# Turning gate columns and a product's operand by DRAM transfers and VectorE block transposes in an mLSTM and feed-forward kernel

## The chip, the core and the metric

The kernel runs on one core of a Trainium2 chip. A core has five engines that work side by side, each with its own queue of instructions in a fixed order: TensorE (PE; matrix products, with weight loads shown apart as PEld), VectorE (DVE), ScalarE (ACT), GpSimd (POOL) and SyncE (SP), which here only starts transfers. Transfers run on DMA engines. Operands lie in SBUF (128 partitions), products arrive in PSUM. The metric is the time of one execution on the device in microseconds.

## What is computed

Two blocks in a row, all in float32: an mLSTM cell with batch 4, 8 heads, 768 steps and head size 40, and a feed-forward block with 320 inputs, 2048 hidden units and 320 outputs on its 3072 rows.

```python
for t in range(S):
    m_new = np.maximum(f_gate[:, :, t] + m, i_gate[:, :, t])
    f_stab = np.exp(f_gate[:, :, t] + m - m_new)
    i_stab = np.exp(i_gate[:, :, t] - m_new)
    m = m_new
    C = f_stab[:, :, None, None] * C + i_stab[:, :, None, None] * np.einsum('bhd,bhe->bhde', vt, kt)
    n = f_stab[:, :, None] * n + i_stab[:, :, None] * kt
    h_tilde = np.einsum('bhde,bhe->bhd', C, qt)
    nq = np.einsum('bhd,bhd->bh', n, qt)[:, :, None]
    denom = np.maximum(np.abs(nq), 1.0)
    o = 1.0 / (1.0 + np.exp(-o_gate[:, :, t]))
    y[:, :, t] = o * h_tilde / denom
x = y.transpose(0, 2, 1, 3).reshape(B * S, H * D)
h = x @ w_in
g = h * (1.0 / (1.0 + np.exp(-1.702 * h)))
return g @ w_out
```

## The kernel before

The 768 steps are cut into six chunks of 128 (`w` = 0 to 5, called chunk 0 to 5 here). The sequential cell becomes, for each chunk, products of 128 by 128 or, from chunk 1 on, of two halves of 64 steps, with a carried state per head (`state`, and `state_mid` between the halves). All instructions are written in the order in which each engine runs them; there is no scheduler, and an engine waits at the head of its queue until its operands are there. All transfers are issued by SP, in program order, and completion counters are shared by every eighth transfer, so at most eight are under way.

The main loop runs over `w`. Each turn has an up stage (`up` for chunk 0, `up_fast` after it: `xT` times `w_in`, eight steps `j`, then GELU) and a down stage (`down`, 16 blocks, for chunk 0; `down_fast`, 14 blocks, after it: the hidden values times `w_out`). Between the blocks of the down stage of chunk `w` stands the attention of chunk `w + 1`, spread by the list `at` in `attention(w)`: a call at entry `i` comes after block `i`. So the attention of chunk 1 runs beside 16 blocks of chunk 0, and those of chunks 2 to 5 beside 14 blocks each. The last chunk has nothing beside its down stage.

The steps of an attention, in order:

- `gates(w)`, early in the up stage before: VectorE scans over the gates with heads on the partitions, stacked in `st` (96 rows: 32 heads by three quantities). From chunk 1 on the two halves of the steps are also copied the other way round into `swapped` (L290), and the decays between halves are spread by `dec` (L297). The running maximum goes to DRAM (`m_row`) and comes back spread over the partitions as `wt` (`spread`, eight transfers, L359).
- `columns(w)`: puts steps on the partitions. TensorE multiplies `st` by `keep` and `swapped` by `swap` (odd heads have their halves exchanged) and `dec` by `half`, into `p_cols` (L316, L317, L323). VectorE copies 32 columns (L326), ScalarE takes exponentials of the rest (L327, L329).
- `scale` (`vw`, L483) and `decay` (L476) on GpSimd; `weights` (32 exponentials on ScalarE, L377, and masks on GpSimd, L381); `carry` (TensorE `p_c` L493, then on VectorE L502, L476, L502 for each half of the heads); `scores` (TensorE `p_s` L401, VectorE L404); `values` (TensorE `p_o` L442 and `p_i` L450, then VectorE L456, L457 and `outputs`, which ends with `y`, L420, and a copy of 64 columns on GpSimd, L423).
- `seam`: TensorE transposes `y` in six pieces for each half of the batch into `p_x` (L466), ScalarE copies them to `xT` (L468).

`token_sums` (L555 to L560) forms sums of `xT` at the start of the next up stage, and `input_sums` (L544 to L547), in chunk 0's down stage only, sums of `w_in`: both are needed since `up_fast` and `down_fast` use seven products of halves where eight would be usual. `hidden_sums` (L663 to L666) and `last_sums` (L672) do the same for the down stage. Every block's result is added up by VectorE into `o_sb` (L690, L692; chunk 0: L640) and stored by SP (L696, L641).

PSUM is held by two pools. `ps_m` has four single banks for blocks and half of the up products. `ps_a` has two bank pairs (`banks(name)`), used in turn by p_cols, p_c, p_s, p_o, p_i, p_x and the rest of the up products; a user waits until the last reader of the pair two allocations before is done.

From chunk 2 on `k` and `q` are loaded as 32-row squares (`load_squares`, tiles `k_sq` and `q_sq`, issued after block 12) and turned by VectorE's block transposes of 32 by 32 (L349, in `block_transposes`). The calls that place all this in the main loop:

```python
at = (0, 1, 3, 4, 8, 9, 10, 11, 13) if w == 1 else (0, 1, 2, 4, 6, 7, 8, 9, 11)
calls = [[(columns, w), (decay, w, 0, 0), (decay, w, 1, 0), (scale, w, 0), (scale, w, 1)],
         [(weights, w, 0)], [(weights, w, 1), (open_gates, w)], [(carry, w, 0), (carry, w, 1)],
         [(scores, w, 0), (scores, w, 1)], [(values, w, 0)], [(values, w, 1)], [(seam, w, 0)], [(seam, w, 1)]]
```

Of the kernel before, what the change touches and what calls it, by code (L numbers as in the profile page):

```python
# [26 lines left out]
def kernel(  # L27
# [73 lines left out]
    def load_squares(w):  # L101
        for dst, src in ((k_sq, k), (q_sq, q)):
# [29 lines left out]
    def piece_in(c, n):  # L132
        return (w_in_sb[:, c, n * 512:(n + 1) * 512],
                [(slice(0, 128), slice(0, 512), w_in_bits[c * 128:(c + 1) * 128, n * 1024:(n + 1) * 1024])])
# [74 lines left out]
    keep, swap = (const.tile([3 * BH, 3 * BH], FP, name=n) for n in ("keep", "swap"))  # L209
    odd = const.tile([3 * BH, 1], FP, name="odd")  # L210
    full = ident[0:3 * BH, 0:3 * BH]

    half = const.tile([BH, 2, 64], FP, name="half")
    par = const.tile([BH, 2], FP, name="par")
    pair = const.tile([BH, BH // 2], FP, name="pair")
    V.tensor_reduce(out=par, in_=ident[0:BH, 0:BH].rearrange("p (j two) -> p two j", two=2), axis=AX.X, op=OP.add)
    V.tensor_reduce(out=pair, in_=ident[0:BH, 0:BH].rearrange("p (j two) -> p j two", two=2), axis=AX.X, op=OP.add)
    V.tensor_copy(out=half, in_=par.unsqueeze(2).to_broadcast([BH, 2, 64]))
# [7 lines left out]
    cols, stacked, m_row, dec = {}, {}, {}, {}  # L226
    kT, qT, ys, xT, gs, o_ps, sums, vw = {}, {}, {}, {}, {}, {}, {}, {}
# [16 lines left out]
    def gates(w):  # L244
# [42 lines left out]
        if w:  # L287
            stacked[w] = st, swapped
            for x in range(2):
                V.tensor_copy(out=swapped[:, x * HL:(x + 1) * HL], in_=st[:, (1 - x) * HL:(2 - x) * HL])  # L290
        if w:
            dec[w] = gate.tile([BH, 2, BH // 2], FP, name="dec")
# [3 lines left out]
            for x in range(2):  # L296
                V.tensor_scalar(out=dec[w][:, x, :], in0=pair, scalar1=both[:, x:x + 1], scalar2=None, op0=OP.mult)  # L297
# [8 lines left out]
    def masks():  # L306
        V.tensor_reduce(out=odd, in_=full.rearrange("p (j two) -> p two j", two=2)[:, 1], axis=AX.X, op=OP.add)
        V.tensor_scalar(out=swap, in0=full, scalar1=odd, scalar2=None, op0=OP.mult)
        V.memset(swap[BH:2 * BH, :], 0.0)
        V.tensor_tensor(out=keep, in0=full, in1=swap, op=OP.subtract)  # L310

    def columns(w):
        pt = banks("p_cols")[:, 0, :]
        st = stacked[w]
        if w:
            T.matmul(pt[:, 0:3 * BH], st[0], keep, start=True, stop=False)  # L316
            T.matmul(pt[:, 0:3 * BH], st[1], swap, start=False, stop=True)  # L317
        else:
            T.transpose(pt[:, 0:3 * BH], st, full)
        n = 3 * BH  # L320
        if w in dec:
            n += BH
            T.matmul(pt[:, 3 * BH:n], half.rearrange("p a b -> p (a b)"), dec[w].rearrange("p a b -> p (a b)"),  # L323
                     start=True, stop=True)
        c = cols[w] = gate.tile([L, 4 * BH], FP, name="cols")
        V.tensor_copy(out=c[:, 0:BH], in_=pt[:, 0:BH])  # L326
        A.activation(out=c[:, BH:3 * BH], in_=pt[:, BH:3 * BH], func=AF.Exp, scale=-1.0)  # L327
        if w in dec:
            A.activation(out=c[:, 3 * BH:n], in_=pt[:, 3 * BH:n], func=AF.Exp)  # L329
# [76 lines left out]
    def outputs(w, hs, u):  # L406
# [16 lines left out]
        G.tensor_copy(out=y[:, :, DM:DM + 64], in_=y[:, :, DM - 64:DM])  # L423
# [36 lines left out]
    def seam(w, c, bs=(0, 1)):  # L460
        if w not in xT:
            xT[w] = work.tile([128, 3, B, L], FP, tag="xT", bufs=1, name="xT")
        px = banks("p_x")[:, 0:len(bs), 0:3 * L]
# [386 lines left out]
```

## Time and profile before

| | value |
|---|---|
| median of three runs (lowest, highest) | 486.65 us (486.65, 486.92) |
| the profiled execution | 486.67 us |
| its span, first to last instruction | 485.0 us |
| granted TensorE clock | 1.00 |
| SP's hardware queue, share of 16 DMA engines | 50.3% |
| up stage of chunk 3, start to end | 270.5 to 303.1 us |
| down stage of chunk 3 | 303.1 to 344.6 us |
| DMA share in that up stage, in that down stage | 1.10, 0.05 |

A line of the profile's groups or timeline names the engine, the source line, what is written and read, shapes, and durations. "Idle before" is time in which the engine had nothing it could start, with the instruction that ended it. The chain of waits is the sequence of work that ended last, followed back from the end. Busy time of TensorE is modelled at the ends of pipelined products, so the chain's pieces are better for sums than the busy times.

### The profile page before, as it was taken

The page shows a single profiled execution, that of the slowest core. Times are in us where ns is not written, and L with a number is a line of the kernel's source. Part 1 is how long each engine was busy: PE and PEld are TensorE (multiplying, and loading weights), DVE is VectorE, ACT ScalarE, POOL GpSimd, SP SyncE. Part 2 cuts the span into 40 slices and gives each one's busy share as a digit, 9 for nine tenths or more (in the row PEclk, how much of TensorE's full clock was granted, in tenths as well). Part 3 has the DMA queues.
Part 4 walks back from the last instruction along what each step waited for, and adds up shares of the span by engine and source line. Part 5 has one row for each costly group of instructions (what it writes and reads, how often), then busy time and mean ns, then how long its engine had stood idle before and what let it go on. Part 6 is the DMA issues. An engine that isn't in the chain of part 4 may idle for free.

```text
span 485.0 us, 12103 instructions
## 1 busy us (share of the span) xinstructions
PE 479.3 (99%) x5016; PEld 388.0 (80%) x5016; DVE 344.0 (71%) x680; ACT 195.3 (40%) x434; POOL 149.7 (31%) x145
## 2 busy tenths in 40 slices
PE   8999999999999999999999999999999999999997
PEld 5774447777767999767999877999876999876997
DVE  6675976988778966768967668968677958343812
ACT  3746557801453901444811354720264630164200
POOL 6020003400398610127620136630035640035300
PEclk9999999999999999999999999999999999999999
DMA  8999995005992000999000899000799000000000
GB/s 176 182 285 146 254 206 153 2 18 103 208 157 45 3 30 3 174 185 139 1 31 3 153 189 158 1 31 3 127 195 165 10 30 3 29 0 1 0 28 27
DMA packets 130790, 44.31 MB, mean 91 GB/s; under 512 B 105616, under 2 KB 128176, under 8 KB 130736
## 3 DMA queue, kind: packets, MB, share of 16 engines
q1 hardware_dynamic: 130736, 43.55, 50.3%
q8 instruction: 39, 0.64, 0.6%
q14 instruction: 15, 0.12, 0.1%
HBM read 39.52 MB, written 4.01 MB: 90 GB/s over the span
## 4 chain that ended last, share of the span: by engine, by line
PE 95%; DVE 3%; POOL 1%; ACT 0%; issue 0%; POOLq 0%; DVEq 0%
PE p_out L687 32%; PE p_h L585 26%; PE p_h L590 8%; PE p_out L636 7%; PE p_h L515 6%; PE p_c L493 3%; PE p_o L442 2%; PE p_s L401 2%; PE p_i L450 2%; PE p_h L521 2%; PE p_x L466 1%; PE p_t L341 1%; PE p_o L432 1%; PE p_s L390 0%; DVE wt L392 0%
## 5 line engine op out<-in xcount | busy, mean ns | idle before, releaser
L627 POOL TENSOR_TENSOR g<-g,parts 128x512 f32<-128x512 f32 x30 | 38.3, 1276 | 124.4 <-DVE parts L619 113.3
L687 PE MATMUL p_out<-w_out_sb,g 128*128 128x160 f32 x480 | 71.0, 302 | 0.0
L687 PEld LDWEIGHTS p_out<-w_out_sb,g 128*128 128x128 f32 x480 | 66.6, 190 | 0.9
L585 PE MATMUL p_h<-xT,w_in_sb 128*128 128x256 f32 x240 | 66.9, 388 | 0.0
L566 ACT ACTIVATE g<-g 128x512 f32<-128x512 f32 x80 | 50.0, 631 | 35.3 <-DVE g L622 24.8
L585 PEld LDWEIGHTS p_h<-xT,w_in_sb 128*128 128x128 f32 x240 | 43.8, 190 | 20.2 <-issue 7.6
L468 ACT COPY xT<-p_x 128x768 f32<-128x768 f32 (+1 forms) x14 | 9.9, 707 | 114.1 <-PE p_x L466 114.1
L692 DVE TENSOR_TENSOR o_sb<-o_sb,p_out 128x160 f32<-128x160 f32 x70 | 21.0, 316 | 44.2 <-PE p_out L687 43.8
L687 PE MATMUL p_out<-t_sb,s 128*128 128x160 f32 x320 | 47.1, 300 | 0.0
L687 PEld LDWEIGHTS p_out<-t_sb,s 128*128 128x128 f32 x320 | 44.4, 190 | 0.2
L618 DVE TENSOR_TENSOR t_x<-p_h,parts 128x256 f32<-128x256 f32 x40 | 16.8, 419 | 38.9 <-PE p_h L590 34.3
L585 PE MATMUL p_h<-t_x,s_in 128*128 128x256 f32 x160 | 41.1, 379 | 0.0
L590 PE MATMUL p_h<-xT,w_in_x 64*128 64x512 f32 x160 | 39.7, 615 | 0.0
L377 ACT ACTIVATE wt<-wt,cols 128x64 f32<-128x64 f32 x160 | 38.8, 338 | 0.0
L423 POOL COPY y<-y 128x128 f32<-128x128 f32 (+1 forms) x14 | 4.0, 285 | 108.7 <-DVE y L420 108.7
L636 PE MATMUL p_out<-w_out_sb,g 128*128 128x320 f32 x128 | 36.3, 437 | 0.0
L585 PEld LDWEIGHTS p_h<-t_x,s_in 128*128 128x128 f32 x160 | 30.4, 190 | 4.1
L615 ACT COPY parts<-p_h 128x256 f32<-128x256 f32 x40 | 14.9, 374 | 45.9 <-PE p_h L585 45.9
L636 PEld LDWEIGHTS p_out<-w_out_sb,g 128*128 128x128 f32 x128 | 23.6, 190 | 9.2 <-DVE w_out_sb L241 0.2
L619 DVE TENSOR_TENSOR parts<-p_h,t_x 128x512 f32<-128x512 f32 x40 | 27.7, 692 | 4.2
L626 ACT COPY g<-p_h 128x512 f32<-128x512 f32 x30 | 17.4, 580 | 30.5 <-PE p_h L590 25.2
L515 PE MATMUL p_h<-xT,w_in_sb 128*128 128x512 f32 x64 | 29.5, 604 | 0.1
(192 smaller groups left out, 897.5 us busy)
## 6 DMA issues: line engine op xcount, KB each, us to landing
wt<-m_row SPq DMA_DIRECT2D x40, 128.0 KB, 4.3
k_sq<-in_k_dram SPq DMA_DIRECT2D x16, 320.0 KB, 5.9
q_sq<-in_q_dram SPq DMA_DIRECT2D x16, 320.0 KB, 10.1
out_dram<-o_sb SPq DMA_DIRECT2D x24, 160.0 KB, 1.8
eo<-in_o_gate_dram SPq DMA_DIRECT2D x5, 640.0 KB, 10.0
bits<-in_moe_w_in_dram SPq DMA_DIRECT2D x6, 512.0 KB, 9.0
v_st<-in_v_dram SPq DMA_DIRECT2D x14, 160.0 KB, 5.2
bits<-in_moe_w_out_dram SPq DMA_DIRECT2D x6, 320.0 KB, 4.8
```

The lines of the kernel that those rows point to most:

```text
L377: A.activation(out=x[:, h, :], in_=x[:, h, :], func=AF.Exp, scale=-1.0, bias=cols[w][:, c * PH + h:c * PH + h + 1])
L515: T.matmul(ph[j][i], w_in_sb[:, c, f * 128:(f + 1) * 128], x[:, c, :], start=(first and c == 0), stop=(not first and c == 1))
L566: A.activation(out=gs[w, j][:, i, :], in_=gs[w, j][:, i, :], func=AF.Gelu_apprx_sigmoid)
L585: T.matmul(out, a, x[n], start=start, stop=stop)
L590: T.matmul(row, w_in_x[r, j, :], rest_x[r, 2, :], start=not late, stop=late)
L618: V.tensor_tensor(out=u2, in0=both[:, 1, right], in1=y[:, left], op=OP.add)
L619: V.tensor_tensor(out=y[:, half_w:3 * half_w].rearrange("p (a t) -> p a t", a=2), in0=flat[:, half_w:3 * half_w].rearrange("p (a t) -> p a ...
L626: A.copy(out=g[:, 0, :], in_=row0)
L627: G.tensor_tensor(out=g0, in0=g0, in1=u, op=OP.add)
L636: T.matmul(po, gs[w, f // 2][:, f % 2, b * L:(b + 1) * L], w_out_sb[:, f, :], start=(f == 0), stop=(f == NF - 1))
L687: T.matmul(po, a(f), b[:, f, :], start=(f == 0), stop=(f == NH - 1))
L692: V.tensor_tensor(out=dst, in0=x, in1=po, op=OP.add)
```

## The change

For chunks 1 to 5 neither the gates' columns nor `xT` are turned by TensorE any more; chunk 0 keeps the old way.

- Columns: `gates` merges `st` and its exchanged halves into one tile by two masks (`odd`, `even`) and stores it to DRAM (`st_row`), with the two decays of each head (`d_row`). `columns_in` reads them back in five transfers in step 4 (chunk 1) or 2 of the up stage, ahead of `spread`. `columns_turn` block-transposes 96 columns on VectorE, at the end of the up stage. `columns` is left with exponentials; `keep`, `swap`, `half`, `pair` and `dec` go.
- Operand: `outputs` stores `y` to DRAM (`x_row`) and `seam_in` reads it in eight transfers into parts of `q_sq`, in 32-row squares, right after each `values`. `seam_turn` block-transposes them into `xT` on VectorE, in two instructions of 512 and 256 columns. So that two 32-column blocks lie side by side, `w_in`'s first 256 rows are loaded even rows first, and chunk 0's `seam` reads `y` with a step of two.
- Order: `at` and `calls` are new. In chunks 2 to 5 `weights`, `carry`, `scores` and `values` stand one or two blocks earlier, and the two `scores` are apart. `scale` precedes `decay`. `q_sq` of a later chunk is loaded after the last `seam_turn`.

```diff
     def gates(w):
...
         if w:
-            stacked[w] = st, swapped
             for x in range(2):
-                V.tensor_copy(out=swapped[:, x * HL:(x + 1) * HL], in_=st[:, (1 - x) * HL:(2 - x) * HL])
-        if w:
-            dec[w] = gate.tile([BH, 2, BH // 2], FP, name="dec")
+                V.tensor_scalar(out=swapped[:, x * HL:(x + 1) * HL], in0=st[:, (1 - x) * HL:(2 - x) * HL], scalar1=odd,
+                                scalar2=None, op0=OP.mult)
+            V.scalar_tensor_tensor(out=swapped, in0=st, scalar=even, in1=swapped, op0=OP.mult, op1=OP.add)
...
-            for x in range(2):
-                V.tensor_scalar(out=dec[w][:, x, :], in0=pair, scalar1=both[:, x:x + 1], scalar2=None, op0=OP.mult)
+            st_row = rows.tile([L // 32, 3 * BH, 32], FP, name="st_row")
+            d_row = rows.tile([BH, 2], FP, name="d_row")
+            stacked[w] = st_row, d_row
+            nc.sync.dma_start(out=st_row.rearrange("n k t -> k n t"), in_=swapped.rearrange("k (n t) -> k n t", t=32))
+            nc.sync.dma_start(out=d_row, in_=both)
...
+    def columns_in(w):
+        st_row, d_row = stacked[w]
+        x = raw[w] = gate.tile([L, 5 * BH], FP, bufs=1, name="raw")
+        for n in range(L // 32):
+            nc.sync.dma_start(out=x[n * 32:n * 32 + 32, 0:3 * BH].rearrange("r (k t) -> r k t", t=32),
+                              in_=st_row[n].rearrange("(k r) t -> r k t", r=BH))
+        nc.sync.dma_start(out=x[:, 3 * BH:], in_=d_row.rearrange("h x -> (h x)").unsqueeze(0).to_broadcast([L, 2 * BH]))
+
+    def columns_turn(w):
+        c = cols[w] = gate.tile([L, 4 * BH], FP, name="cols")
+        V.transpose(out=c[:, 0:3 * BH].rearrange("p (k h) -> p k h", h=BH),
+                    in_=raw[w][:, 0:3 * BH].rearrange("p (k t) -> p k t", t=32))
...
+        c = cols[w]
+        A.activation(out=c[:, BH:3 * BH], in_=c[:, BH:3 * BH], func=AF.Exp, scale=-1.0)
+        d = raw[w][:, 3 * BH:].rearrange("p (j i x) -> p i x j", i=2, x=2)
+        for i in range(2):
+            r = slice(i * 64, i * 64 + 64)
+            A.activation(out=c[r, 3 * BH:].rearrange("p (x j) -> p x j", x=2), in_=d[r, i], func=AF.Exp)
...
         y = ys[w, c][:, b:b + n // H]
-        G.tensor_copy(out=y[:, :, DM:DM + 64], in_=y[:, :, DM - 64:DM])
+        if w == 0:
+            G.tensor_copy(out=y[:, :, DM:DM + 64], in_=y[:, :, DM - 64:DM])
+            return
+        x = x_row[w, c] = rows.tile([2 * L, DM], FP, name="x_row")
+        nc.sync.dma_start(out=x.rearrange("(b t) d -> t b d", b=2), in_=y[:, :, 0:DM])
...
+    def x_square(c, n):
+        at, m = (c * 768, 64) if n == 0 else (c * 768 + 512, 32)
+        return q_sq[:, at:at + 8 * m].rearrange("r (b y) -> r b y", y=m)
+
+    def seam_in(w, c):
+        x = x_row[w, c].rearrange("(b r) d -> r b d", r=32)
+        for n, m in ((0, 64), (1, 32)):
+            for g in range(4):
+                at = g * 64 if n == 0 else 256 + g % 2 * 32
+                nc.sync.dma_start(out=x_square(c, n)[g * 32:g * 32 + 32], in_=x[:, :, at:at + m])
+
+    def seam_turn(w, c):
+        for n, k in ((0, slice(0, 2)), (1, slice(2, 3))):
+            V.transpose(out=x_of(w)[:, k, 2 * c:2 * c + 2, :].rearrange("p c b (n r) -> p (b n) c r", r=32),
+                        in_=x_square(c, n).rearrange("p b (d c) -> p b c d", d=32))
...
-        at = (0, 1, 3, 4, 8, 9, 10, 11, 13) if w == 1 else (0, 1, 2, 4, 6, 7, 8, 9, 11)
-        calls = [[(columns, w), (decay, w, 0, 0), (decay, w, 1, 0), (scale, w, 0), (scale, w, 1)],
+        at = (0, 1, 3, 4, 8, 8, 9, 10, 12, 14) if w == 1 else (0, 0, 1, 3, 4, 5, 5, 6, 9, 12)
+        calls = [[(columns, w), (scale, w, 0), (scale, w, 1), (decay, w, 0, 0), (decay, w, 1, 0)],
                  [(weights, w, 0)], [(weights, w, 1), (open_gates, w)], [(carry, w, 0), (carry, w, 1)],
-                 [(scores, w, 0), (scores, w, 1)], [(values, w, 0)], [(values, w, 1)], [(seam, w, 0)], [(seam, w, 1)]]
+                 [(scores, w, 0)], [(scores, w, 1)], [(values, w, 0), (seam_in, w, 0)], [(values, w, 1), (seam_in, w, 1)],
+                 [(seam_turn, w, 0)], [(seam_turn, w, 1)]]
...
             if w + 2 < NW and i == 13:
-                load_squares(w + 2)
+                load_squares(w + 2, "kq" if w else "k")
+            if w == 0 and i == 15:
+                load_squares(w + 2, "q")
             block()
             run(side.get(i, []))
```

## The prediction

> **What bounds the kernel now.** First the page's head and slices, for the engine without idle time.
>
> ```profile
> span 485.0 us, 12103 instructions
> PE 479.3 (99%) x5016; PEld 388.0 (80%) x5016; DVE 344.0 (71%) x680; ACT 195.3 (40%) x434; POOL 149.7 (31%) x145
> PE   8999999999999999999999999999999999999997
> DVE  6675976988778966768967668968677958343812
> PEclk9999999999999999999999999999999999999999
> ```
>
> TensorE is busy in every slice at full clock: what it no longer does is gained, unless something else makes it wait. Next, the chain of waits in one stage, chunk 3's down products with chunk 4's attention between them (columns: start, us, what).
>
> ```profile
> 303.12 2.17 PE p_out L687 x16
> 305.29 0.20 PE p_cols L316 x2
> 305.49 0.22 PE p_cols L317 x2
> 305.71 0.33 PE p_cols L323 x2
> 306.04 8.89 PE p_out L687 x64
> 314.93 2.01 PE p_c L493 x128
> 316.94 4.54 PE p_out L687 x32
> 321.48 2.02 PE p_s L401 x128
> 334.63 0.66 PE p_x L466 x6
> 339.64 0.66 PE p_x L466 x6
> ```
>
> The chain never leaves TensorE; what the change removes (p_cols, p_x) lies on it. Third, VectorE's timeline in the same stage, to see how far it runs behind.
>
> ```profile
> 311.21 4.62 DVE L672 TENSOR_TENSOR s<-g,s 128x256 f32<-128x256 f32 x4
> 315.75 0.97 DVE L692 TENSOR_TENSOR o_sb<-o_sb,p_out 128x160 f32<-128x160 f32 x3
> 317.23 1.38 DVE L476 TENSOR_TENSOR state<-state_mid,cols 128x328 f32<-128x328 f32 x1
> 318.64 0.50 DVE L502 TENSOR_TENSOR state<-p_c,state 128x328 f32<-128x328 f32 x1
> 336.52 1.49 DVE L672 TENSOR_TENSOR s<-g,s 128x256 f32<-128x256 f32 x4
> ```
>
> Block 3 left TensorE at 312.8 and is read at 315.8. VectorE is 3 us behind and without a pause from 303 to 321 (17.3 of 18 us busy by the windows). Four equal L672 take 4.62 us here, while GpSimd works, and 1.49 us at 336, when it rests. TensorE does not notice: four ps_m buffers lie between them, and p_s, at 321.48, finds its bank pair free since 319.1, the end of the L502 at 318.64.
>
> **What is removed.** In each of five chunks: 12 p_x transposes, 2 x 0.66 = 1.32 us, and p_cols, 0.20+0.22+0.33 = 0.75 us. Sum 2.07, times 5: -10.3 us. The block after an interlude costs 0.2 more than the others (2.37 against 2.17, L687); one interlude (p_cols) goes, one comes (scores are split from chunk 2 on), so 0. ACT loses two copies of 0.80 (L468) and GpSimd two of 0.29 (L423), both idle then: 0.
>
> **What is added and hidden.** `gates` swaps two copies and two small products (0.19, 0.22) for three operations of such sizes, and the columns' block transpose is 96 of the 512 columns of L349 (1.12 us), 0.2, against the 0.18 copy L326: 0, since VectorE is busy 25.5 of 32.6 us in that stage; without that cover about 0.3 a chunk. SP gets 7 more DMAs in the up stage, ahead of wt's eight. At 0.41 (fi) to 0.73 each (wt, issued 294.3 to 300.2) wt lands 3 to 5 us later than 304.5 (300.1 + 4.4). ACT reads its first half from 309.3, the second 3.9 later: hidden; without cover, ACT's 7.7 us of L377 start late and L404 with them.
>
> Two seam turns of 512 and 256 columns cost VectorE 1.12+0.56 each, 3.4 a chunk, in the stage's last third, where it is busy 8.8 of 14.6 us. I take 0 for the work itself; bounds 0 and 3.4.
>
> By the rows a transpose of 128 columns costs TensorE 0.11 us (0.66 for six) and VectorE 0.28, on an engine with room, so only what TensorE waits for counts. A rule speaks against the change: the Trainium skill, "VectorE: DVE Perf Modes", Rules for kernel authors, sends 128x128 transposes to TensorE where PSUM may receive them. Were VectorE's time charged in full, as that rule would have it, the sum would be 5 x 3.4 - 10.3 = +6.7, about 493 us.
>
> **First wait: scores behind the carry, chunks 2 to 5.** The scores of the first half move from after block 6 to after block 4. Their bank pair is that of the first half's p_c (two pairs take turns), free when VectorE has done its last L502. TensorE gets there at 303.12 + 4 x 2.17 + 2.01 + 2.37 = 316.2. VectorE has the same queue ahead (L665, L666, L663, blocks 0 to 2, L672), only block 4's two additions (0.65) fall behind it; the columns' turn adds 0.2, the copy's end gives 0.1, and the L663 pair now overlaps GpSimd's vw fully (0.68 against 1.1), +0.4. So 319.1 - 0.65 + 0.1 + 0.4 = 318.9, wait 2.7 us. Bounds: 2.0, if L663 stays and L476 takes its short 0.50 row; 3.2, if both stretch. Then L404 of the second half ends some 0.3 after the second interaction product wants its bank: 0.3 (0 to 0.5). Together 2.9 in chunks 2 to 4 (2.0 to 3.7). Chunk 5 carries one state, so L476 and a L502 are missing (1.9): 0.8 + 0.2 = 1.0 (0 to 1.5). Sum 3 x 2.9 + 1.0 = +9.7. Queued behind: every later block of the stage, on TensorE.
>
> **Second wait: the way through DRAM.** y is stored, then read by eight DMAs that wait for the store. Store: 1.8 us to landing for out's 160 KB, I take 2.0 for 320 KB. Issues: 0.41 (fi) to 0.63 (wt); I take 0.47, near k_sq's 0.49 at twice the rows, so 3.8 for eight. Landing of the last 2.0 (bounds 1.8 of out and 2.9, the quickest of m_row and wt).
>
> Chunk 1 (stage 76.30 to 122.01): 2.07 and an interlude's 0.2 less put TensorE's end at 119.8. Second y, 113.85 now, comes 0.9 earlier, 112.9; the first at 108.6. Store lands 110.6, reads issue until 114.4; SP, in order, stores the second then, landed 116.4, reads until 120.2, landed 122.2. VectorE holds at that turn. Behind it stand, in program order, the second half of the turn (0.56), input_sums (117.49 to 120.10 now: 2.6), block 15's copy (0.41) and the first token sum (0.45).
>
> ```profile
> 119.42 0.68 DVE L547 TENSOR_TENSOR s_in<-w_in_sb,s_in 128x512 f32<-128x512 f32 x1
> 122.05 0.49 DVE L640 COPY o_sb<-p_out 128x320 f32<-128x320 f32 x1 [1.95 <-PE p_out L636]
> 122.46 0.42 DVE L555 TENSOR_TENSOR t_x<-xT 128x256 f32<-128x256 f32 x1
> ```
>
> So input_sums, which now ends 1.9 us before TensorE is done, ends at 125.4, and the sum at 126.2. The up product's fourth factor needs it at 119.8 + 3 x 0.43 = 121.1: +5.1 us. Bounds: three landings in series at 1.8 and sixteen issues at 0.41 give 3.5, at 2.9 and 0.63 give 10.4; I take 5.1, nearer the low end, since these transfers find the DMA engines idle as out's do.
>
> Chunks 2 to 5: the second values product is after block 6, seven blocks (15.3 us) from the end. With the first wait in it, the first y is ready at 329.8 and the second at 334.2; the first is read until 335.7, out's store(0) goes at 335.7 and lands at 337.5 (VectorE waits for it with block 8's sum, 3 us, while four PSUM buffers carry TensorE up to block 12), the second lands at 343.8. Its turn ends at about 345.1, TensorE's blocks at 345.3, the token sum at 346.0 against 346.6 needed: 0, with 0.6 to spare. At a landing of 2.9 three in series are 2.7 later: 2.1 a chunk. The next q_sq load waits for this turn; block transposes want it 16 us later.
>
> No pause of TensorE exceeds 1.1 us here and the granted clock is 1.00 throughout, so what a pause of 5 us does to the clock no row shows. The Trainium skill, "TensorE: Matmul & The Clock Gate", Part 1, halves the array's clock after an idle window of about 3.4 us, for about as long again. By that page the forecast would be 1.7 us more, 492.9.
>
> **Sum.** -10.3 + 9.7 + 5.1 = +4.5: span 489.5. The profiled execution took 486.67 with a span of 485.0, 1.67 outside it; the median of the runs is 486.65, the same. Forecast 491.2 us.
>
> **Rivals.**
> Faster: GpSimd's new order lets L672 run free. If scale, decay and the masks are through when VectorE reaches it, four take 1.5 to 2 us, the bank is free before TensorE asks, and the 9.7 shrinks to about 1: 482.5. For it: GpSimd starts about 1 us earlier. Against: its six operations still take until 318 (1.46, 0.95, 1.25 each), past L672. It decides from where the four take less than 3.1 us, 1.5 off each of three chunks.
>
> Nothing waits: full 10.3, 476.4. It needs the chunk 1 turn before 118, against 122.2 from the shortest rows but one: small.
>
> Slower still: landings near 2.9, since 128 and 256 byte rows are packets as small as wt's. Then chunk 1 pays 5.1 + 3 x 0.9 = 7.8 and chunks 2 to 5 about 2 each: 485 - 10.3 + 9.7 + 7.8 + 8.4 + 1.7 = 502.3; half way there is 496.7. Against: DMAs are idle then (share 0.05).
>
> **How the numbers follow.** Forecast 0.60, free L672 or a shorter wait 0.20, nothing waits 0.05, late landings 0.15. The forecast's own bounds: 485 - 10.3 + 6.0 + 3.5 + 1.7 = 485.9 to 485 - 10.3 + 12.6 + 7.8 + 1.7 = 496.8 (the issues at 0.63 left out, since nothing else is in the queue). The range takes in the faster rival's upper part and half of the late landings: 482.5 to 497.5. A measurement tells 0.2%, 1 us, from no change: faster below 485.7 is the faster rivals less a little, 0.23; same 0.06 from the forecast's low end; slower 0.71.
>
> **What would show it.** p_x and p_cols gone after the first chunk; TensorE idle 2 to 3 us ahead of the first p_s in chunks 2 to 4, released by VectorE's L502 line, and less in chunk 5; about 5 us at the first up product after chunk 1, ended by VectorE's sums, with the turn itself waiting for DMA. Wrong if p_s starts without a pause or if the turn's data lands before 118.

## The result and the profile after

| | before | after |
|---|---|---|
| median of the runs (lowest, highest), us | 486.71 (486.65, 486.92) | 502.1 (500.57, 503.64) |
| ratio, 95% interval | 1 | 1.0315 (1.0282 to 1.0349) |
| the profiled execution, its span, us | 486.67, 485.0 | 501.56, 499.8 |

The change makes the kernel 3.2% slower. The forecast was 491.2 us, with 497.5 as the upper end of its range: the direction was right, the size was not.

The page of the changed kernel, with the rows that answer to those shown of before:

```profile
span 499.8 us, 12087 instructions
PE 475.9 (95%) x4926; PEld 380.7 (76%) x4926; DVE 352.4 (71%) x691; ACT 190.2 (38%) x429; POOL 149.1 (30%) x135
PE   8999999997799989999989999989999999999997
PEclk9999999999799999999999999999999999999999
```

TensorE, which had no hole, now has them: a wide one in the slices from 112 us on, where the granted clock also falls, and a shallow one in each later chunk. Its waits (us in total, times, longest):

```profile
PE p_h L615 <- DVE t_x L585: 5.4, 2, 4.4
PE p_s L405 <- DVE state L532: 3.6, 3, 1.2
PE p_out L717 <- DVE g L693: 3.5, 4, 0.9
PE p_h L615 <- DVE xT L498: 2.1, 1, 2.1
PE p_i L458 <- DVE wt L408: 1.4, 4, 0.4
PE p_i L458 <- issue: 1.4, 2, 0.9
```

In the line numbers of after, L615 and L620 are the up products, L717 the down products (chunk 0: L666), L405 the scores, L450 and L458 the values, L532 the carry on VectorE, L693 to L696 and L702 the sums of hidden values, L498 the seam's block transposes, L585 the first token sum.

Cutting both traces at the first up product and the first down product of each chunk gives a ledger (us, worked out from the timelines):

| stage | 0 up | 0 down | 1 up | 1 down | 2 up | 2 down | 3 up | 3 down | 4 up | 4 down | 5 up | 5 down |
|---|---|---|---|---|---|---|---|---|---|---|---|---|
| before | 42.05 | 45.71 | 32.79 | 41.52 | 32.63 | 41.53 | 32.63 | 41.53 | 32.63 | 41.51 | 32.63 | 33.70 |
| after | 42.05 | 44.24 | 41.57 | 43.85 | 32.63 | 43.41 | 32.64 | 42.67 | 33.04 | 41.72 | 34.14 | 33.71 |

A chunk's attention runs in the down stage of the chunk before: chunk 1's in "0 down", chunk 5's in "4 down". The start of chunk 1 costs 8.78 us, four down stages that were to become shorter by about 2 became longer by 2.33, 1.88, 1.14 and 0.21, and the up stages of chunks 4 and 5 grew by 0.41 and 1.51.

What happens ahead of chunk 1's up stage is in two timelines of after. First SyncE's queue (start, us, what):

```profile
109.43 0.39 SPq L431 DMA_DIRECT2D x_row<-y  x1
112.08 3.78 SPq L494 DMA_DIRECT2D q_sq<-x_row  x8
115.96 1.46 SPq L431 DMA_DIRECT2D x_row<-y  x1
119.40 3.76 SPq L494 DMA_DIRECT2D q_sq<-x_row  x8
```

Then VectorE's:

```profile
122.84 0.71 DVE L498 STREAM_TRANSPOSE xT<-q_sq 128x512 f32<-128x512 f32 x1 [3.44 <-DMA q_sq<-x_row]
124.83 0.45 DVE L498 STREAM_TRANSPOSE xT<-q_sq 128x256 f32<-128x256 f32 x1 [1.28 <-DMA q_sq<-x_row]
125.20 0.65 DVE L574 TENSOR_TENSOR s_in<-w_in_sb 128x512 f32<-128x512 f32 x1
...
127.70 0.48 DVE L670 COPY o_sb<-p_out 128x320 f32<-128x320 f32 x1
128.10 0.41 DVE L585 TENSOR_TENSOR t_x<-xT 128x256 f32<-128x256 f32 x1
```

The second store goes out only after the eight reads of the first half, at 115.96. VectorE stands idle for 3.44 and 1.28 us at the turn, then has to do `input_sums` (L574 to L577), and reaches the sum that TensorE wants at 128.10. In the stretches around it (PE busy, PEld, DVE, ACT, POOL; then granted clock, DMA share, GB/s):

```profile
124.00:126.00 2.00, 0.30 (x2) 0.00 (x0) 1.13 (x3) 0.00 (x0) 0.00 (x0) 0.98 0.75 190
126.00:128.00 2.00, 0.00 (x0) 0.00 (x0) 2.00 (x4) 0.00 (x0) 0.00 (x0) 0.50 1.20 208
130.00:132.00 2.00, 2.00 (x6) 1.35 (x4) 1.84 (x7) 0.00 (x0) 0.00 (x0) 0.50 1.18 192
132.00:134.00 2.00, 2.00 (x9) 0.86 (x8) 1.65 (x9) 0.32 (x1) 0.00 (x0) 0.82 1.18 245
```

When TensorE comes out of the second pause, at 128.7, it works at half its clock until 132.7. The two pauses (2.12 and 4.35) make 6.5 of the 8.78 us; the other 2.3 are put down to the clock, which e4 below tests.

At the end of chunk 5's attention the chain of waits runs through the transfers themselves:

```profile
416.46 2.94 DMA x_row<-y
...
423.78 4.09 DMA x_row<-y
...
431.26 2.00 DMA q_sq<-x_row
...
434.04 0.34 DVE t_x L585
434.38 0.14 issue
434.52 2.17 PE p_h L615 x8
```

The first half's last reads and a store of the result (L726) were issued within a microsecond ahead of the second store; whether they make it last 4.09 us is not shown. TensorE waits 1.07 us for the first token sum here, where the prediction had 0.6 to spare.

### The profile page after: what moved, and what is told of

Same layout as the page of the kernel before. It is cut to its first block, busy times and chain, and to the rows that moved or that the text cites. A ratio compares the mean times of both kernels' runs of the same rounds, so it can differ in the third digit from the quotient of the medians.

```text
span 499.8 us, 12087 instructions
## 1 busy us (share of the span) xinstructions
PE 475.9 (95%) x4926; PEld 380.7 (76%) x4926; DVE 352.4 (71%) x691; ACT 190.2 (38%) x429; POOL 149.1 (30%) x135
## 5 line engine op out<-in xcount | busy, mean ns | idle before, releaser
L717 PE MATMUL p_out<-w_out_sb,g 128*128 128x160 f32 x480 | 70.7, 302 | 3.5 <-DVE g L693 3.5
L717 PEld LDWEIGHTS p_out<-w_out_sb,g 128*128 128x128 f32 x480 | 66.8, 190 | 5.5 <-DVE g L693 4.5
L615 PE MATMUL p_h<-xT,w_in_sb 128*128 128x256 f32 x240 | 67.4, 390 | 0.0
L596 ACT ACTIVATE g<-g 128x512 f32<-128x512 f32 x80 | 49.9, 631 | 32.8 <-DVE g L652 26.3
L615 PEld LDWEIGHTS p_h<-xT,w_in_sb 128*128 128x128 f32 x240 | 44.0, 191 | 20.4 <-ACT g L656 10.6
L615 PE MATMUL p_h<-t_x,s_in 128*128 128x256 f32 x160 | 42.2, 387 | 5.4 <-DVE t_x L585 5.4
L717 PE MATMUL p_out<-t_sb,s 128*128 128x160 f32 x320 | 47.1, 300 | 0.0
L717 PEld LDWEIGHTS p_out<-t_sb,s 128*128 128x128 f32 x320 | 44.4, 190 | 0.2
L620 PE MATMUL p_h<-xT,w_in_x 64*128 64x512 f32 x160 | 39.9, 617 | 0.0
L615 PEld LDWEIGHTS p_h<-t_x,s_in 128*128 128x128 f32 x160 | 30.6, 193 | 10.7 <-issue 6.5
L666 PE MATMUL p_out<-w_out_sb,g 128*128 128x320 f32 x128 | 36.0, 436 | 0.7 <-DVE w_out_sb L234 0.7
L513 POOL TENSOR_TENSOR vw<-v_st,cols 128x656 f32<-128x656 f32 x12 | 18.9, 1591 | 57.6 <-DMA t_sb<-in_moe_w_out_dram 44.2
L666 PEld LDWEIGHTS p_out<-w_out_sb,g 128*128 128x128 f32 x128 | 23.8, 190 | 10.6 <-DVE w_out_sb L234 1.2
L652 DVE TENSOR_TENSOR g<-p_h,parts 128x512 f32<-128x512 f32 x40 | 27.6, 691 | 1.4
```

The source lines that it names most:

```text
L513: G.tensor_tensor(out=vw[w, c], in0=v_st[:, hs, :], in1=e, op=OP.mult)
L596: A.activation(out=gs[w, j][:, i, :], in_=gs[w, j][:, i, :], func=AF.Gelu_apprx_sigmoid)
L615: T.matmul(out, a, x[n], start=start, stop=stop)
L620: T.matmul(row, w_in_x[r, j, :], rest_x[r, 2, :], start=not late, stop=late)
L652: V.tensor_tensor(out=g[:, 1, :], in0=row1, in1=y[:, half_w:3 * half_w], op=OP.add)
L666: T.matmul(po, gs[w, f // 2][:, f % 2, b * L:(b + 1) * L], w_out_sb[:, f, :], start=(f == 0), stop=(f == NF - 1))
```

## The experiments

All times below are medians; the ratio with its 95% interval is to the kernel before in the same session. Down stages are numbered as in the ledger.

**e1: the columns alone.** The operand goes back to TensorE, calls and order are those of before; only the columns go through DRAM.

```diff
-        at = (0, 1, 3, 4, 8, 8, 9, 10, 12, 14) if w == 1 else (0, 0, 1, 3, 4, 5, 5, 6, 9, 12)
+        at = (0, 1, 3, 4, 8, 9, 10, 11, 13) if w == 1 else (0, 1, 2, 4, 6, 7, 8, 9, 11)
...
-                 [(seam_turn, w, 0)], [(seam_turn, w, 1)]]
+                 [(seam, w, 0)], [(seam, w, 1)]]
```

> Columns through DRAM in chunks 1 to 5, xT by TensorE again, attention in the order and at the places of before. If the columns' way costs nothing: 5 x (0.75 + 0.2) less than 486.7, less the 0.7 us wait for w_out that the changed kernel shows in chunk 0: 482.6 us. If GpSimd's earlier start by itself stretches the late hidden sums (L693 in the changed kernel, 3.24 us for two against 1.83 of L663 before), block 3 waits some 0.9 us in four chunks: about 486.

Measured: 484.96 us, 0.9966 (0.9953 to 0.9979). The expectation, 482.6, was missed by 2.4 us. The down stages beside chunks 2 to 4 fall to 40.92, by 0.6 each, where p_cols with the block behind it had cost 0.95. The rest goes to two short waits: the 29th and the 61st down product of such a stage each come 0.15 us late. What they read comes from ScalarE's GELU (L596) and from VectorE's L693, and these end only 0.05 us before; in the kernel before, p_cols stood ahead of these products and hid the waits. Nothing of the columns' transfers is waited for. Chunk 0's stage falls by 0.11 only, since a wait of 0.68 for `w_out_sb` takes p_cols' place; stage 4, beside chunk 5 (41.51), not at all: TensorE stops there for 0.36 us, of which more below. This half of the change is a small gain.

**e2: the new order without the operand's way.** As e1, with after's order of calls.

```diff
-        at = (0, 1, 3, 4, 8, 9, 10, 11, 13) if w == 1 else (0, 1, 2, 4, 6, 7, 8, 9, 11)
-        calls = [[(columns, w), (decay, w, 0, 0), (decay, w, 1, 0), (scale, w, 0), (scale, w, 1)],
+        at = (0, 1, 3, 4, 8, 8, 9, 10, 11, 13) if w == 1 else (0, 0, 1, 3, 4, 5, 5, 6, 9, 11)
+        calls = [[(columns, w), (scale, w, 0), (scale, w, 1), (decay, w, 0, 0), (decay, w, 1, 0)],
...
-                 [(scores, w, 0), (scores, w, 1)], [(values, w, 0)], [(values, w, 1)], [(seam, w, 0)], [(seam, w, 1)]]
+                 [(scores, w, 0)], [(scores, w, 1)], [(values, w, 0)], [(values, w, 1)],
+                 [(seam, w, 0)], [(seam, w, 1)]]
```

> As the one before, but with the changed kernel's order of the attention (scores after blocks 4 and 5, scale ahead of decay), xT still by TensorE. If the earlier scores are what costs in the down stages of chunks 1 to 4: the waits of the changed kernel, 0.9 (hidden sums), 1.2 (p_s) and 0.35 (p_i) a chunk with 0.6 to 1 more of small ones, so 2.5 to 3.4 us more than columns alone in three chunks, about 1 in the fourth: 8 to 10 us above the first run. If instead the transfers and turns of xT cause these waits: no more than 2 us above it.

Measured: 501.82 us, 1.0314 (1.0297 to 1.0331): the order alone, with no transfer of `y`, costs 16.9 us over e1. Its down stages beside chunks 2 to 4 are 45.83, 46.27 and 45.67. Besides the waits for L532, L693 and L408, which are those of after to 0.1 us, TensorE stops in `p_i` for nothing that the trace shows (its timeline; in brackets the idle time before, "issue" where no releaser is seen):

```profile
178.39 0.31 PE L458 MATMUL p_i<-state_mid,qT 40*64 40x41 f32 x2 [0.76 <-issue]
183.24 0.19 PE L458 MATMUL p_i<-state,qT 40*64 40x41 f32 x1 [0.40 <-issue]
257.15 0.19 PE L458 MATMUL p_i<-state_mid,qT 40*64 40x41 f32 x1 [1.10 <-issue]
262.03 0.25 PE L458 MATMUL p_i<-state_mid,qT 40*64 40x41 f32 x1 [0.52 <-issue]
335.36 0.25 PE L458 MATMUL p_i<-state,qT 40*64 40x41 f32 x1 [0.32 <-issue]
340.30 0.19 PE L458 MATMUL p_i<-state_mid,qT 40*64 40x41 f32 x1 [0.60 <-issue]
```

They come in pairs 4.85 to 4.94 us apart, and in each pair 126 or 127 product records lie between the two.

**e3: the sums ahead of the turn.** After, with the second `input_sums` ahead of the second turn in chunk 0's down stage.

```diff
             block()
+            if w == 0 and i in (11, 14):
+                input_sums(slice(0, 4) if i == 11 else slice(4, 8))
             run(side.get(i, []))
...
-            if w == 0 and i in (11, 14):
-                input_sums(slice(0, 4) if i == 11 else slice(4, 8))
```

> The changed kernel with the last input_sums ahead of chunk 1's second turn instead of behind it. If VectorE's order behind the late transfer makes the long pause before the up products of chunk 1: the first token sum comes 2.4 us earlier, 499.7; up to 2.3 more if the clock then stays up, 497.4. If the transfer alone sets the pause: unchanged, 502.1.

Measured: 499.21 us, 1.0257 (1.0241 to 1.0273). This is near the 499.7 expected. Chunk 1's up stage falls from 41.57 to 39.72: the queue behind the turn is a real part of the second wait.

**e4: idle products in the two pauses.** After, with 8 and 18 idle products in chunk 1's first up step.

```diff
             product(2, row0[:, left], late, False)
+            busy(8)
...
             row_0()
+            busy(18)
         product(5, both[:, 1, left], True, True)
```

> The changed kernel with 8 and 18 idle products (0.22 us each) put into the two pauses of the first up step of chunk 1, where nothing else can run. If the half clock after the pause (0.50 from 126 to 132 us) costs time: 2 to 2.3 us less, 499.8 to 500.1, clock 1.00 there. If not: 502.1 or a little more.

Measured: 503.46 us, 1.0352 (1.0325 to 1.0379). The clock stays at 1.00 from 124 to 134 and chunk 1's up stage falls by 2.0, to 39.57: that is the price of the clock. But the down stages after it, where nothing was changed, rise to 44.30, 44.57 and 45.02, and the whole gets no faster. Ahead of those stages stand 26 products more in TensorE's code, and its stops without a releaser grow from two (1.4 us) to six (3.9 us).

**e5: the stores from another queue.** After, with `y` stored from ScalarE's queue.

```diff
-        nc.sync.dma_start(out=x.rearrange("(b t) d -> t b d", b=2), in_=y[:, :, 0:DM])
+        nc.scalar.dma_start(out=x.rearrange("(b t) d -> t b d", b=2), in_=y[:, :, 0:DM])
```

> The changed kernel with the store of y to DRAM issued from ScalarE's queue instead of SP's. If the second store of a stage is late because it stands in SP's order behind the eight reads of the first: in chunk 1 it starts about 3 us earlier (at about 113 instead of 115.96), the first up step after chunk 1 loses about 3 of its 6.5 us of pauses, and the 1.07 us at chunk 5's first up step vanish: 497.6 us, and 495.3 if the shorter pause also keeps the granted clock up. If what holds the data is the transfers themselves and not the order of issue: the second transfer only becomes longer and the time stays within 1 us of 502.1.

Measured: 497.71 us, 1.0228 (1.0206 to 1.025). In chunk 1 the sixteen reads now follow each other (SyncE's queue of e5):

```profile
111.79 9.17 SPq L494 DMA_DIRECT2D q_sq<-x_row  x16
```

They end at 120.96 instead of 123.16, chunk 1's up stage is 39.13, and those of chunks 4 and 5 are back at 32.63: their 0.41 and 1.51 us go with the late store. The store did stand behind the reads in the queue's order. The pause of 4.3 us and the clock's fall remain. In the profiled execution stage 4 is longer than in after, 43.95 against 41.72: TensorE stops for 0.58 us in `p_i`, and behind that the granted clock is 0.50 from 410.2 to 413.6.

**e6: GpSimd's order.** e2 with decay ahead of scale.

```diff
-        calls = [[(columns, w), (scale, w, 0), (scale, w, 1), (decay, w, 0, 0), (decay, w, 1, 0)],
+        calls = [[(columns, w), (decay, w, 0, 0), (decay, w, 1, 0), (scale, w, 0), (scale, w, 1)],
```

> The columns-only kernel with the new order (501.82 us), but GpSimd's decay ahead of its scale again, as before the change. If the 0.9 us that the first down product of each later stage waits for VectorE's L693 comes from GpSimd's order (scale now overlaps L693): four of these waits vanish, 3.6 us less, 498.2. If it comes from where the calls stand: unchanged within 1 us. In both cases the waits of p_s for L532 (3.7 us) stay.

Measured: 501.23 us, 1.0297 (1.0271 to 1.0323), a miss in size. The wait for L693 is gone, so GpSimd's order did make it; but a new one stands in its place (waits of e6):

```profile
PE p_s L405 <- DVE state L532: 4.1, 3, 1.4
PE p_c L523 <- POOL vw L513: 2.5, 8, 0.3
```

The carry, one block earlier than before the change, needs `vw`, which is now last. In both orders that were run with the carry at that place, one of the two is paid.

**e7: the scores late.** e2 with scores and values at their places of before.

```diff
-        at = ... else (0, 0, 1, 3, 4, 5, 5, 6, 9, 11)
+        at = ... else (0, 0, 1, 3, 6, 6, 7, 8, 9, 11)
```

> The columns-only kernel with the new order (501.82 us), but in chunks 2 to 5 the scores stand after block 6, and the values after 7 and 8, as before the change. If the early, split scores and the small products standing close behind each other cost the time: the waits of p_s (3.7 us), of p_i for its weights (1.3) and at issue (3.7) vanish, 8.7 us less, about 493, and 489.5 if the waits of the first down product (3.5) were a consequence of the same crowding. If it is the earlier weights and carry or GpSimd's order: it stays above 499.

Measured: 489.3 us, 1.0054 (1.0039 to 1.0069): 12.5 us of the new order's 16.9 come from where scores and values stand, stops included. The waits for L532 and L408 are gone and of the issue waits one (0.7) is left; what remains over e1 is the wait for L693 (3.5) and that.

**e8: half of the operand.** e1's order, the first half of the operand through DRAM and VectorE, the second by TensorE.

```diff
+                 [(scores, w, 0), (scores, w, 1)], [(values, w, 0), (seam_in, w, 0)], [(values, w, 1)],
+                 [(seam_turn, w, 0)], [(seam, w, 1)]]
```

> The columns-only kernel with the order of before (484.96 us), where also the first half of the up product's operand goes through DRAM and VectorE's block transposes, and the second half stays with TensorE. The first half's data is needed some 5 blocks after its store, so it should not be waited for: five p_x groups of 0.66 us less, 3.3 us, and about 0.3 us more where VectorE's turn delays its queue: 481.6 to 483. If VectorE's queue is full at that place (its turn, 1.15 us, ahead of the block sums of the last third): no gain, 484.5 to 486.

Measured: 485.11 us, 0.9968 (0.9956 to 0.9979), no gain over e1, though no wait for the operand's data is left. The time is the one expected if VectorE's queue were full at the turn, but e11 below has the same turns and is 3.2 us faster. The chain of e8, beside chunk 3's attention:

```profile
246.37 1.90 PE p_s L405 x117
248.26 0.50 issue
248.76 0.45 PE p_s L405 x11
```

The scores, 2.02 us in e1, take 2.85. The stage takes 41.29; chunk 5's, without such a stop, 40.22.

**e9, e10, e11: the code's place.** e2 and e8 with 64, and e8 with 16, products more in TensorE's code, ahead of everything and in time where it waits for the first data. The narrow ones write 16 columns; 2 wide and 70 narrow, or 7 and 17, stand for the 8 wide ones.

```diff
-    keep_busy(8)
+    keep_busy(2)
+    for _ in range(70):
+        T.matmul(p_idle[:, 0:16], idle, idle[:, 0:16], start=True, stop=True)
```

> The columns-only kernel with the new order (501.82 us), with 64 products more in TensorE's code, ahead of all work (2 wide and 70 narrow idle products in place of 8 wide ones, in time where TensorE waits for the first data). If the issue waits (3.7 us in six, 126 or 128 products apart in each stage) are TensorE's code arriving in blocks of 128 products with their weight loads, what lies between two blocks' ends changes everywhere: the waits of chunks 2 to 4 move or vanish, chunk 5's order gets the place that chunks 2 to 4 have now, and the time changes by 1.5 to 6 us, more likely down. If they come from data, semaphores or the order of the work: the same waits at the same products and the time within 0.7 us.

> The kernel with half of the operand through DRAM (485.11 us), with 64 products more in TensorE's code ahead of all work. Its p_s of chunks 2 to 4 stops at issue after 117 of 128 products, p_i too, and these stages take 41.29 to 41.86 us; chunk 5's, whose code is 64 products shorter ahead of p_s, has no such wait and takes 40.22. If the code's place decides: chunks 2 to 4 get chunk 5's 40.2 and chunk 5 their 41.3, 3 us less, 482. If not: unchanged within 0.7 us.

> The same kernel with 16 products more in TensorE's code ahead of all work. If the code's place decides, the wait at issue in p_s of chunks 2 to 4 comes 16 products earlier, after 101 of 128 instead of after 117. If it belongs to the work, it stays after 117. The time: within 2 us of 485.11 in both cases.

Measured: e9 501.12 us, 1.0297 (1.0281 to 1.0312); e10 484.34, 0.9946 (0.9926 to 0.9966); e11 481.89, 0.9902 (0.9882 to 0.9922), with no edit to the work. The totals of e9 and e10 move by 0.7 and 0.8 us only, which is near what was expected if the place played no part, and e11's moves by 3.2, more than was expected either way (e11 is the median of two executions, 481.74 and 482.03). The stages, each taken from one execution, say more than the sums:

| down stage | 0 | 1 | 2 | 3 | 4 |
|---|---|---|---|---|---|
| e2 | 45.60 | 45.83 | 46.27 | 45.67 | 42.75 |
| e9 (e2, 64 more) | 48.77 | 44.05 | 44.06 | 44.06 | 44.60 |
| e8 | 44.91 | 41.86 | 41.29 | 41.56 | 40.22 |
| e10 (e8, 64 more) | 46.54 | 40.25 | 40.23 | 40.24 | 40.22 |
| e11 (e8, 16 more) | 44.92 | 40.24 | 40.23 | 40.24 | 40.37 |

The stops in the stages 1 to 3 vanish in all three, and those stages become equal to 0.02 us; in e9 and e10 others appear in the stages 0 and 4, or 0. What was expected of chunk 5 in e10 (its stage to rise to 41.3) did not come, and e11's stop did not move to product 101: it vanished. That the place in the code decides, and not the data, is shown, and the traces also say which places: the last section counts them. The same stretch of e10 (line numbers are 2 higher):

```profile
247.71 2.02 PE p_s L407 x128
```

**e12: the changed kernel at another place.** After with the 16 products.

> The changed kernel (502.1 us) with 16 products more in TensorE's code ahead of all work. If the place of the code decides part of its loss: its waits at issue (1.4 us in two) and the lengthened products beside them move, and the time changes by 1 to 5 us; the waits for L532, L693 and the seam's data stay. If the place plays no part in this kernel: within 0.7 us of 502.1, and all of the loss is in the waits for VectorE and the data.

Measured: 504.65 us, 1.0377 (1.0355 to 1.0399): 2.5 us more, within the range expected. In the profiled execution the down stages 1 to 3 are longer, 45.64, 43.80 and 43.72, and chunk 5's up stage is shorter, 32.89 against 34.14; the waits for L534 (3.7) and L695 (3.5), after's L532 and L693, stay. Stage 1 does not pay for its stop (1.03 us) alone: behind it the granted clock is 0.50 from 186.9 to 190.3.

**e13, e14: a mended version, misplaced.** Both halves through DRAM, each mechanism mended: scores a block after the carry and together, decay first, stores and half of the reads from ScalarE's queue, the sums ahead of the turn.

```diff
+        at = (0, 1, 3, 4, 8, 9, 10, 13, 15) if w == 1 else (0, 1, 2, 4, 5, 6, 7, 11, 13)
...
+                (nc.sync, nc.scalar)[g % 2].dma_start(out=x_square(c, n)[g * 32:g * 32 + 32], in_=x[:, :, at:at + m])
```

> Both halves of the operand through DRAM, as in the change, but with the calls of chunks 2 to 5 at blocks 0, 1, 2, 4, 5, 6, 7, 11, 13 (scores together, one block after the carry), GpSimd's decay first, y stored from ScalarE's queue, the eight reads split over SyncE's and ScalarE's queues, and input_sums ahead of the second turn. If each mechanism found so far is the one that costs: no p_s, L693 or seam wait, the down stages beside chunks 2 to 4 take 40.92 - 1.36 = 39.6 us, U1 32.8: 478.2, and up to 4 more where the code's place is bad. If the way through DRAM is too long even so: 1 to 2 us of wait at the start of each up stage, 484 to 488.

> The same with 16 products more in TensorE's code ahead of all work. If the code's place matters, it differs from the one without by 1 to 4 us, either way; the better of the two is at 478 to 480.

Measured: 561.75 and 564.52 us. The second turn here stands behind the next chunk's load of `q` into the same buffer, so it turns `q` and waits for that load; nothing else can be read from these times.

**e15: the columns alone at e11's place.**

> The columns-only kernel with the order of before (484.96 us) with the same 16 products more. It has one wait at issue (0.36 us, in chunk 5, whose stage takes 41.5 against 40.9 in the others), so little can be gained by place: 484.3 to 485, or up to 3 more if the new place is bad for chunks 2 to 4. Against it, e11 with half the operand through DRAM (481.89) shows what that half is worth at the same place: 0.68 us in each of five chunks.

Measured: 485.66 us, 0.9983 (0.9973 to 0.9992). Stages 1 to 3 stay at 40.91; stage 4 has the stops (42.65). In stages 1 to 3, where neither kernel stops, e11 is 0.67 us shorter: one p_x group (0.68), as forecast from its row.

**e16, e17: the mended version.** e13 and e14 with the load after the turn.

> As e13_mended, with the next chunk's k and q loaded after the second seam turn (e13 loaded q into the turn's buffer ahead of it, so that its last third turned and waited for other data). If the mechanisms found so far are all: no p_s, L693 or seam wait in the stages, down stages beside chunks 2 to 4 at 39.6 us, U1 32.8: 478.2, and up to 4 more where the code's place is bad. If the way through DRAM is too long even so: 1 to 2 us of wait at the start of each up stage, 484 to 488.

> The same as e16 with 16 products more in TensorE's code ahead of all work. If the code's place matters, it differs from e16 by 1 to 4 us, either way; the better of the two is at 478 to 480 if the way through DRAM is short enough.

Measured: 495.75 us, 1.018 (1.0163 to 1.0197), and 500.0, 1.0278 (1.0263 to 1.0294). Both are far above what was expected: the mending doesn't suffice. Scores one block after the carry still wait for L532 (4.4 us in five waits in e16), each up stage after chunk 1's takes 33.54 instead of 32.63 because the turn is late, chunk 1's still 37.63. The two differ by 4.25 us though the place of the code is all that was changed; in e17's trace the granted clock is 0.50 in the down stages 1 to 3 for 13.7 us together, in e16's for 3.4. In e16's stage 4, the only one that neither waits nor stops, the 39.6 expected are there: 39.54.

The fastest of all is e11: half of the operand off TensorE, the order of before, and a place of the code at which no dense stretch stops: 481.89 us against 486.67, the median of two executions.

## Why the prediction was wrong

The mechanism it put forward, waits that eat the gain, is the one that acts, and the two large waits stand where it said. What failed is the sum: it took too much for the work removed and too little for the second wait, put the clock and the ends of chunks 2 to 5 at nothing, and has no term for TensorE's code. Term by term (span of after less span of before, in us; the measured values come from the ledger and the group starts of after's timeline, one execution of each kernel):

| term | forecast | measured |
|---|---|---|
| work removed | -10.3 | -8.2 |
| first wait and what stands with it | +9.7 | +10.1 |
| second wait, at chunk 1 | +5.1 | +6.5 |
| the clock behind it | 0 | +2.3 |
| end of chunks 2 to 5 | 0 | +1.9 |
| TensorE's code | not foreseen | +2.3 |
| sum | +4.5 | +14.9 |

- *Removed work.* The p_x and p_cols groups are gone at the durations of their rows. But a chunk gained 0.4 us less: stage 3, which has no stop, takes 42.67, and 39.84 without its waits of 0.88, 1.21 and 0.74, which is 1.69 less than the 41.53 of before, not 2.07. The interludes are not the reason. "One goes, one comes" is even too strict: the second half's scores stand next to the first values, so that five blocks of a stage stand behind an interlude in before and four in after. What came out from behind p_cols are waits: in stage 3 the four blocks ahead of the carry take 10.12 us, where 4 x 2.17 and the wait of 0.88 make 9.56. The 29th product waits there for ScalarE's GELU, and those up to the 61st for L693, as in e1. In chunk 0 it is the wait of 0.68 for `w_out_sb`.
- *First wait.* 2.83 a chunk against 2.9, by another division. In the fourth block of the stage, at the 61st product (not at the first, as e6's expectation has it), TensorE waits 0.88 for L693, which the prediction did not have: after's timeline of VectorE shows the pair at 3.24 us beside GpSimd's `vw` and the four L702 at 3.92:

```profile
320.64 3.24 DVE L693 TENSOR_TENSOR g<-g 128x512 f32<-128x512 f32 x2
...
324.26 3.92 DVE L702 TENSOR_TENSOR s<-g,s 128x256 f32<-128x256 f32 x4
```

  "Scale first" moved the overlap from L702, which TensorE did not feel, to L693, which it does. TensorE is then later at `p_s`, which waits 1.21 instead of 2.7, and the second half's scores (L408, 1.22 us) hold `p_i` by 0.74 instead of 0.3 (the prediction made 2.9 of its 2.7 and 0.3). When VectorE is through with the carry was right: `p_s` starts 15.8 us after the stage's first down product, where the prediction has 15.9 (318.9 less 302.95). That is in part luck, since the pair takes longer than it was given and the four L702 less. In chunk 5 the sum is 1.6 against 1.0. The faster rival, L672 (now L702) running free, did not come: 3.92 us is above its limit of 3.1.
- *Second wait.* The chain (store, reads, second store behind them, reads, turn, `input_sums`, sum) is the one forecast, and e5 and e3 show two of its links. It was mis-sized: the first store left at 109.4 and not at 108.6, the two stores of chunk 1 landed after 2.6 and 3.4 us where 2.0 was taken (median of all ten: 2.5), and the sum was done at 128.5, not at 126.2. The eight reads took the 3.8 us that were forecast.
- *The clock.* The text gave 1.7 us for it by the Trainium skill, "TensorE: Matmul & The Clock Gate", Part 1, and left it out of the sum. The trace agrees with the page that the clock halves: it is 0.50 after the pause of 4.4 us. From the end of the pause it stays so for 4.1 us, which makes 2.0; e4 got 2.0 back in that stage. The 2.3 of the table is what the pauses leave of the stage's 8.78 us, and 0.3 of it stays unexplained.
- *End of chunks 2 to 5.* "0, with 0.6 to spare" failed by the landing: 2.94 and 4.09 us for chunk 5's stores. This is the rival "slower still", whose full price, 502.3, is close to the measured time by accident: it put 8.4 us at these ends, where 1.9 were found. With the store in another queue (e5) both late up stages, chunk 4's and chunk 5's, are back at 32.63.
- *TensorE's code.* The step that is missing altogether. A move of small products closer together was counted as a move of waits only. e2, e9, e10, e11, e15, e16 and e17 show that it has a price of its own, 1.6 to 2.2 us a stage (stages 1 to 3 of e2 less those of e9), which depends on where in the code the products stand. In after it is 1.18 and 0.74 us in the stages 1 and 2, by their excess over stage 3, and 0.36 in stage 4, by the length of `p_i` (1.42 against 1.06). That stage 3 pays nothing fits e9: its stages without a stop take 44.05, which is after's 42.67 and two p_x groups (0.68 each).

What the change gains at best is shown by the parts: 0.6 us a chunk for the columns (e1), 0.67 for the first half of the operand (e11 against e15), and some 1.4 for both halves (e16's stage 4, 39.54, against the 40.92 of e1's stages 1 to 3). What it pays is the room that the longer way needs: to have `y` two blocks earlier, scores and values move up against the carry, and that costs more (e7: 12.5 us, waits and stops together) than all ten p_x groups give (two a chunk at 0.66, 6.6).

Left open: what starts the transfer of a block of code, so that it could be told beforehand which place stops; why the granted clock falls behind some stops; and whether some order keeps both halves off TensorE without a loss.

## What to carry to other kernels

When an operand is sent a longer way round, price first the room that the order must make for it, at the place where the moved work comes to stand; the way itself may be the smaller cost. A store should not stand in one queue behind the reads of an earlier store, which wait for that store to land: moving the stores to another engine's queue, one word of code, gave 4.4 us back here. And when a stage changes its time though nothing in it was edited, compare it at two places of the code before explaining it by its data.

## What the hardware showed unexpectedly

TensorE can run out of instructions. The page of e2 has, among its queues (packets, MB, share):

```profile
q8 instruction: 39, 0.64, 0.5%
```

39 packets of 16.4 KB; TensorE's some 5000 products and as many weight loads make 39 groups of 256 as well, and e9, with the most products of all, shows 40. The traces have each packet's time. A few of the stops that have no releaser, with the packet that ended last before TensorE went on (us), and the number of product records ahead of the stop, counted from the start of the program:

| stop | packet, start to end | TensorE goes on | records ahead |
|---|---|---|---|
| e9, `p_s` | 100.12 to 101.22 | 102.71 | 852 |
| e8, `p_s` | 172.07 to 173.00 | 174.29 | 1609 |
| e17, `p_s` | 175.36 to 176.32 | 177.69 | 1609 |
| e2, `p_i` | 175.43 to 177.18 | 178.39 | 1736 |
| e12, `p_i` | 183.39 to 184.33 | 185.72 | 1736 |
| after, `p_i` | 187.62 to 188.70 | 190.31 | 1863 |

So it is for every one of the 52 stops of 0.2 us or more in the traces of this case: it ends 1.2 to 1.6 us after such a packet, and it lies at one of the same places in the code, which are 126 or 127 product records apart, whatever the kernel does there. Some records are missing from a trace, so that 128 products, which are 256 instructions with their weight loads, fit the distance. Extra products shift the work against these places. In e11 the place 1609 is product 101 of `p_s`, as was expected; it does not stop there because its packet has ended 4.4 us before. In the kernel before, which has no stop, each packet has ended at least 2.1 us before TensorE comes to its place. What makes a packet start early or late is not shown.

Two stops that follow each other at neighbouring places lie 3.75 to 5.5 us apart, in stretches where 128 products of 40 or 64 rows need only 2.0 us by themselves; 128 of the large down products need 17. The Trainium skill, "Runtime: NRT & Kernel Launch", Instruction fetch mechanics, has code arrive in blocks of 256 instructions and calls the cost of crossing from one to the next mostly hidden. The packets and the places agree with the blocks; the cost is hidden here where large products stand, and is 0.2 to 1.3 us a stop where small ones do.

The granted clock can fall without a long pause. In e5, e6, e12, e16 and e17 it is 0.50 for 3.4 or 6.8 us in a down stage in which TensorE never waits longer than 1.4 us. Part of the scatter between executions of one kernel goes with the clock: after's slowest, 503.64 us, has a mean of 0.986, the profiled one 0.993.

A block transpose on VectorE was cheaper than its row of before: 0.71 and 0.45 us for 512 and 256 columns, against 1.12 for 512 there.
